# Attention on 128 partitions: 64x32 score products with keys on partitions, and softmax results turned in 32x32 blocks by VectorE

## The chip, the cores and the metric

The kernel runs on one core of one Trainium2 chip. The metric is device time in microseconds from start to end of one execution; the profile shows one execution, and times of several executions stand beside it.

## What is computed

```python
def sm_attn(qq, kk, vv):                  # softmax over the last axis
    s = scale * np.matmul(qq, kk.transpose(0, 1, 3, 2))
    a = np.exp(s - np.max(s, axis=-1, keepdims=True))
    a = a / (np.sum(a, axis=-1, keepdims=True) + 1e-09)
    return np.matmul(a, vv)
# q, k, v: 4 batches, 8 heads, 576 tokens, 64;  p: 4, 8, 32, 64
p_packed = sm_attn(p, k, v)               # 32 packed rows a head
x = sm_attn(q, p_packed, p_packed)        # heads side by side: 2304 x 512
h = x @ w_in                              # 512 x 2048
x = (np.maximum(h, 0) + np.log1p(np.exp(-np.abs(h)))) @ w_out    # 2048 x 512
gate = 1 / (1 + np.exp(-(x @ w_gate)))    # 512 x 1536
out = (gate * (x @ w_val)) @ w_out2       # 1536 x 512
```

All inputs arrive in DRAM: q, k, v, p in float32, the weights in float64.

## The kernel before, in words

The program has three parts that overlap. **Attention** is cut into eight units: unit `u` is batch `u // 2` and half of its heads (four heads). A unit is a Python generator (`attn_unit`) whose `yield`s divide it into 11 stages; `att_tick` moves one unit on by one stage, and up to three units are in flight. **The first expert layer** goes by batch, 256 columns of `w_in` at a time: `emit_h` multiplies, `emit_out1` adds the second product into the tile `xa`, and between its pieces `between` calls `att_tick` and `tick` (one step of weight preparation). The later batches' attention therefore stands between the first batches' products in TensorE's order. **The second expert layer** follows.

Large products split each float32 operand into two float32r parts, so one product is three matmuls (L111 to L113, L641 to L644). Products of the attention, and the transposes, are plain float32; one such matmul is two records in the trace, a transpose one.

A unit before: tokens stand on 96 partitions, six tokens each. GpSimd puts two heads side by side (`by_chunk`, L336), TensorE transposes chunks of 96 tokens (L347), ScalarE copies them out of PSUM (L354). The scores of p (L378) have the 128 rows of four heads' p on partitions and use a left operand with zeros off a head's own block. After the softmax, TensorE turns the result (L412), ScalarE copies it (L413), and 24 products with v (L431) give the packed rows, which ScalarE puts into `bdT`. The scores of q (L455) have tokens on partitions. Their softmax runs in two halves on 96 partitions: VectorE takes the maximum, subtracts, sums and inverts (L465 to L472), ScalarE does the exponential (L469), GpSimd the product (L473). TensorE turns the result (L483), ScalarE and VectorE split it into `A2h` and `A2l`.

The second product of the attention is folded into `w_in`: `Wp` is the packed rows times `w_in` for one batch and 256 columns. `prep_wp_one` (L560) makes it for one batch on 64-column pieces, for columns 0 and 1; `prep_wp_two` (L578) makes it for a pair of batches at once, for columns 2 to 7, and there ScalarE copies to SBUF and GpSimd does both parts of the split (L102, L99).

A weight tile arrives on SyncE's queue (`load_next`) and is converted by three VectorE instructions (L178, L183, L187). Loads of q, k and v (`load_kqv`, L233) take places in `xa` by a table. The order of instructions on each engine is set when the program is built, and each engine runs its own in order; a wait holds up all that stands behind it. The PSUM has four tiles of one bank (`bank1`) and two of two banks (`bank2`).

Of the kernel before, what the change touches and what calls it, by code (L numbers as in the profile page):

```python
# [9 lines left out]
F32 = mybir.dt.float32  # L10
# [10 lines left out]
def attn_moe_moe_kernel(  # L21
# [28 lines left out]
    NC = 6  # L50
    CT = S // NC
# [9 lines left out]
    BAT = (0, 7)  # L61
    ECS = 3
# [5 lines left out]
    VCH = 8  # L68
    VSP = 0
# [13 lines left out]
    # The layers' sums; queries, keys and values before those.  # L83
# [37 lines left out]
    # A weight's float64 words come as pairs of int32, in tiles of 512 columns.  # L121
# [6 lines left out]
    # Some of the second layer's are converted during the first and kept in DRAM.  # L128
# [13 lines left out]
    def load_next():  # L142
# [3 lines left out]
        if XR and key == ("out", 0, 0):  # L146
            # The sums' tile is free until the first of them.
            t = xa[:, : 2 * DM].bitcast(I32).rearrange("p (n t) -> p n t", t=2)
        else:
            t = raw.tile([P, KD * P, 2], I32, tag="raw", name="raw_" + nm)  # L150
        a = c * CF + f * P
        if nm in ("out", "o2"):
            nc.sync.dma_start(t.rearrange("p n t -> p (n t)"), w32[nm][a : a + P, :])
        else:
# [37 lines left out]
    def convert_split(key, pool, shape, tag, bufs):  # L192
# [8 lines left out]
    # Queries, keys and values take the accumulators' slots before those are  # L201
    # needed; a slot's next tile is loaded behind its last use.
    PLACE = {
        0: "345", 1: "621", 2: "345", 3: "634", 4: "563", 5: "456",
        6: "565", 7: "656",
    }
    plan = deque(
        (nm, u, int(s)) for u in range(2 * B) for nm, s in zip("kqv", PLACE[u])
    )
    if PO:  # L210
        first = sorted((plan.popleft() for _ in range(6)), key=lambda x: PO.index(x[0] + str(x[1])))
        plan.extendleft(reversed(first))
    kqv, busy = {}, {}
    KQV = 4 * NC * D

    def load_kqv():
        while plan and plan[0][2] not in busy:
            nm, u, tag = plan.popleft()
            b, g = divmod(u, 2)
            if tag == 6:  # L220
                t = att.tile([CT, KQV], F32, tag="acc6", name=f"{nm}{u}")
            else:
                t = xa[:CT, KQV * tag : KQV * (tag + 1)]
            src = {"k": k, "q": q, "v": v}[nm][b, 4 * g : 4 * g + 4]
            if nm == "v" and u >= VCH:
                t = t.rearrange("p (c h d) -> p c h d", c=NC, h=4)
                for hh in range(4):
                    nc.sync.dma_start(t[:, :, hh], src[hh].rearrange("(r c) d -> r c d", c=NC)) if VSP else None
                if not VSP:
                    nc.sync.dma_start(t, src.rearrange("h (r c) d -> r c h d", c=NC))  # L230
            else:
                t = t.rearrange("p (h c d) -> p h c d", h=4, c=NC)
                nc.sync.dma_start(t, src.rearrange("h (r c) d -> r h c d", c=NC))  # L233
# [35 lines left out]
    for t in pT:  # L269
        nc.gpsimd.memset(t, 0.0)  # L270
# [87 lines left out]
    def attn_unit(u):  # L358
# [119 lines left out]
        for _ in range(BLANK):  # L478
            yield
# [567 lines left out]
```

## Time and profile before

| | |
|---|---|
| time, median of three executions | 874.96 us (873.7 to 875.31) |
| span of the profiled execution | 870.4 us |
| TensorE busy (matmul records) | 841.8 us, 97% |
| VectorE busy | 618.2 us, 71% |
| ScalarE busy | 401.8 us, 46% |
| GpSimd busy | 473.4 us, 54% |

The span runs from the first to the last instruction of the one execution that was profiled; no time of its own is given for that execution. The three timed executions lie 3.3 to 4.9 us above the span. Busy time is the union of an engine's records; a TensorE record is longer than the distance to the next one, since matmuls overlap.

### The profile page before, as it was taken

How to read it: one execution, taken by the hardware profiler on the slowest of the kernel's cores; microseconds unless marked ns; L12 is line 12 of the kernel's file. 1: busy time of each engine (PE TensorE's matmuls, PEld its weight loads, DVE VectorE, ACT ScalarE, POOL GpSimd, SP SyncE). 2: the span in 40 equal slices, each digit the busy share in tenths (PEclk: the TensorE clock that was granted, in tenths of full speed). 3: DMA queues.
4: the chain of work that ended last, by engine and by line, in shares of the span. 5: the costliest groups of instructions: out<-in, count | busy, mean ns of one | idle time of the engine just before them, and what ended most of it. 6: DMA issues, size and time to landing. Idle time of an engine off the chain costs nothing.

```text
span 870.4 us, 15541 instructions
## 1 busy us (share of the span) xinstructions
PE 841.8 (97%) x6064; PEld 790.2 (91%) x6064; DVE 618.2 (71%) x1047; ACT 401.8 (46%) x721; POOL 473.4 (54%) x455
## 2 busy tenths in 40 slices
PE   6889999999999999999999999999989999999997
PEld 5778989989999999999989999999979999999995
DVE  2886556747476857758798688898898746667665
ACT  4557565656666656677633431232342432322210
POOL 4544333254646455476469787886983534436400
PEclk9979999999999999999999999999999999999999
DMA  9774320112032402310056555644424213213004
GB/s 242 197 207 113 83 66 19 49 49 73 25 98 91 134 1 98 110 43 1 2 154 193 162 168 153 188 128 150 153 75 143 82 47 92 67 43 109 14 1 109
DMA packets 58010, 85.55 MB, mean 98 GB/s; under 512 B 6353, under 2 KB 39249, under 8 KB 57937
## 3 DMA queue, kind: packets, MB, share of 16 engines
q1 hardware_dynamic: 57648, 84.49, 33.8%
q8 instruction: 48, 0.79, 0.4%
q14 instruction: 26, 0.20, 0.1%
q10 hardware_dynamic: 288, 0.07, 0.0%
HBM read 65.67 MB, written 18.87 MB: 97 GB/s over the span
## 4 chain that ended last, share of the span: by engine, by line
PE 81%; DVE 9%; DMA 3%; ACT 3%; POOL 2%; issue 1%; SPq 0%; DVEq 0%; ACTq 0%; POOLq 0%
PE bank L113 9%; PE bank L112 9%; PE bank L111 9%; PE ps L641 6%; PE ps L642 6%; PE ps L644 6%; PE ps L967 5%; PE ps L965 5%; PE ps L966 5%; PE ps L113 3%; PE ps L111 3%; PE ps L112 3%; PE ps L578 2%; PE ps L455 2%; DVE aop L99 2%
## 5 line engine op out<-in xcount | busy, mean ns | idle before, releaser
L111 PE MATMUL bank<-aop,BH 128*128 128x288 f32 x672 | 198.7, 296 | 2.8 <-DVE work L918 1.0
L112 PE MATMUL bank<-aop,BH 128*128 128x288 f32 x672 | 197.9, 295 | 1.0 <-DVE aop L99 0.9
L113 PE MATMUL bank<-aop,BL 128*128 128x288 f32 x672 | 198.7, 296 | 0.1
L99 POOL TENSOR_TENSOR ghl<-g,ghl 128x576 fp32r<-128x576 f32 x64 | 93.7, 1465 | 138.8 <-ACT ghl L106 134.4
L649 DVE TENSOR_TENSOR xa<-xa,ps 128x288 f32<-128x288 f32 x224 | 98.1, 449 | 76.9 <-PE ps L644 76.8
L641 PE MATMUL ps<-ghl,woh 128*128 128x288 f32 x512 | 149.2, 306 | 2.5 <-DVE xa L649 2.4
L642 PE MATMUL ps<-ghl,wol 128*128 128x288 f32 x512 | 143.9, 296 | 0.0
L111 PEld LDWEIGHTS bank<-aop,BH 128*128 128x128 f32 x672 | 126.2, 188 | 8.0 <-issue 1.2
L112 PEld LDWEIGHTS bank<-aop,BH 128*128 128x128 f32 x672 | 126.4, 188 | 5.1 <-DVE aop L99 1.6
L113 PEld LDWEIGHTS bank<-aop,BL 128*128 128x128 f32 x672 | 126.5, 188 | 0.4 <-POOL BL L99 0.4
L99 POOL TENSOR_TENSOR BL<-cv,BH 128x512 fp32r<-128x512 f32 (+1 forms) x96 | 117.6, 1241 | 7.2 <-ACT BH L106 6.1
L644 PE MATMUL ps<-ghl,woh 128*128 128x288 f32 x512 | 109.4, 295 | 0.0
L641 PEld LDWEIGHTS ps<-ghl,woh 128*128 128x128 f32 x512 | 96.9, 189 | 6.1 <-DVE xa L649 2.1
L642 PEld LDWEIGHTS ps<-ghl,wol 128*128 128x128 f32 x512 | 97.0, 190 | 0.5
L918 DVE TENSOR_TENSOR work<-work,bank 128x576 f32<-128x576 f32 (+1 forms) x100 | 71.0, 725 | 29.0 <-PE bank L113 28.4
L965 PE MATMUL ps<-oh,gv 128*128 128x512 f32 x216 | 84.6, 392 | 1.3 <-DVE xa L973 0.8
L966 PE MATMUL ps<-ol,gv 128*128 128x512 f32 x216 | 84.8, 393 | 0.0
L967 PE MATMUL ps<-oh,gv 128*128 128x512 f32 x216 | 84.7, 393 | 0.0
L644 PEld LDWEIGHTS ps<-ghl,woh 128*128 128x128 f32 x512 | 82.7, 189 | 0.0
L973 DVE TENSOR_TENSOR xa<-xa,ps 128x512 f32<-128x512 f32 x90 | 61.5, 683 | 27.4 <-PE ps L967 26.9
L947 ACT ACTIVATE work<-bank 128x576 f32<-128x576 f32 (+1 forms) x25 | 15.8, 633 | 137.2 <-DVE bank L918 137.2
L113 PE MATMUL ps<-A2h,wpl 128*128 128x288 f32 x256 | 76.3, 298 | 2.9 <-POOL wpl L99 2.0
(121 smaller groups left out, 1745.8 us busy)
## 6 DMA issues: line engine op xcount, KB each, us to landing
cv<-B SPq DMA_DIRECT2D x52, 256.0 KB, 2.7
B<-cv SPq DMA_DIRECT2D x48, 256.0 KB, 2.9
raw_in<-in_moe_w_in_dram SPq DMA_DIRECT2D x16, 512.0 KB, 4.0
raw_out<-in_moe_w_out_dram SPq DMA_DIRECT2D x16, 512.0 KB, 3.7
raw_g<-in_moe_w_gate_dram SPq DMA_DIRECT2D x12, 512.0 KB, 4.1
raw_v<-in_moe_w_val_dram SPq DMA_DIRECT2D x12, 512.0 KB, 4.4
raw_o<-in_moe_w_out_dram SPq DMA_DIRECT2D x12, 512.0 KB, 4.2
xa<-in_q_dram SPq DMA_DIRECT2D x6, 576.0 KB, 6.6
```

Of the source, the lines that this page charges most:

```text
L99: eng.tensor_tensor(lo, x, hi.bitcast(F32), op=ALU.subtract)
L111: nc.tensor.matmul(ps, wh, xh, start=first, stop=False)
L112: nc.tensor.matmul(ps, wh, xl, start=False, stop=False)
L113: nc.tensor.matmul(ps, wl, xh, start=False, stop=last)
L641: nc.tensor.matmul(out_, wh[:, ms], gh[:, f], start=f == 0, stop=False)
L642: nc.tensor.matmul(out_, wl[:, ms], gh[:, f], start=False, stop=False)
L644: nc.tensor.matmul(out_, wo_hl[c, f][0][:, ms], gl[:, f], start=False, stop=f == 1)
L649: nc.vector.tensor_tensor(dst, dst, out_, op=ALU.add)
L918: nc.vector.tensor_tensor(to, x, y, op=ALU.add)
L965: nc.tensor.matmul(bank, gh[:, ts_], oh, start=f == 0, stop=False)
L966: nc.tensor.matmul(bank, gh[:, ts_], ol, start=False, stop=False)
L967: nc.tensor.matmul(bank, gl[:, ts_], oh, start=False, stop=f == 1)
```

## The change

Tokens now stand on 128 partitions: four heads by 32 groups of 18 tokens. A load of q, k or v is one run of 1152 numbers per partition (18 tokens), and the loads' places are taken from whatever is free, two extra tiles included. TensorE transposes 128x128 chunks (18 a unit for q and k together, where there were 24); two tokens of 64 lie in one chunk, so the halves of the partitions (`e`) hold even and odd tokens. Scores of p and of q are eight products of a 64x32 left operand each (`scores`): the four heads go to four groups of 32 output partitions, and the two halves `e` read different halves of the input partitions and write different banks. Both score tiles have the 32 keys on partitions. VectorE turns 32x32 blocks (`nc.vector.transpose`): once after the first softmax (in place of L412 and L413), once ahead of the second and once behind it (in place of L483). The second softmax runs in one piece of 128x576. The product with v is 72 products of 32 rows each in place of 24 of 96; the packed rows lie in `ppT` without zeros. `Wp` is made of 64x32 pieces too (`prep_wp`), eight for a batch and 256 columns, for a pair of batches at once except at the very first; it takes two banks, and VectorE does the second part of the split in all cases. The split of `A2l` goes from VectorE to GpSimd, `by_chunk` and the zero fills go away. A tile of `w_in` arrives in two DMAs. An output tile of 128 tokens is written by four DMAs of 32 rows each in place of two or three. The stages of a unit stay 11; `BLANK` goes, a second unit now starts at stage 2 of the first (`G0`), and what is needed ahead of a stage (`NEEDS`) is renumbered.

```diff
-    NC = 6
-    CT = S // NC
+    NR = 32
+    NC = S // NR // 2
...
+        elif nm == "in":
+            for g in range(2):
+                nc.sync.dma_start(
+                    t[64 * g : 64 * g + 64].rearrange("p (k n) t -> p k (n t)", k=KD),
...
-                nc.sync.dma_start(t, src.rearrange("h (r c) d -> r h c d", c=NC))
+            nc.sync.dma_start(t, src.rearrange("h (r c) d -> (h r) (c d)", r=NR))
...
+    def turned(src, dst):
+        for i in range(0, NC, 3):
             ps = bank1()
+            for c in range(i, i + 3):
                 nc.tensor.transpose(
+                    ps[:, (c - i) * P : (c - i + 1) * P], src[:, c * P : (c + 1) * P], ident
                 )
+            o = dst[:, i : i + 3].rearrange("p c n -> p (c n)")
+            nc.scalar.activation(o, ps[:, : 3 * P], AF.Copy)
+            yield
...
+    def scores(lhsT, xT, to):
+        for e in range(2):
+            r = slice(64 * e, 64 * e + 64)
+            for h in range(4):
+                n = slice(NK * h, NK * h + NK)
+                nc.tensor.matmul(
+                    to[e][n], lhsT(r, h), xT[r, :, n], start=True, stop=True
+                )
...
+        nc.vector.tensor_scalar(a1, a1, mx[:, 3:4], None, op0=ALU.mult)
+        a1T = att.tile([P, 2 * NC, NK], F32, tag="a1T", bufs=2, name="a1T")
+        nc.vector.transpose(a1T.rearrange("p c n -> p (c n)"), a1)
...
+        pp = [bank1() for _ in range(2)]
+        for e in range(2):
             for c in range(NC):
+                for h in range(4):
+                    r = slice(NR * h, NR * h + NR)
                     nc.tensor.matmul(
+                        pp[h // 2][64 * (h % 2) : 64 * (h % 2) + 64, :NK],
+                        vt[r, c, e, :], a1T[r, e * NC + c, :],
+                        start=e == c == 0, stop=(e, c) == (1, NC - 1),
...
+        for h in range(4):
+            for x in range(2):
+                copy(
+                    PPA[h // 2], ppT[64 * x : 64 * x + 64, b, 4 * g + h, :],
+                    pp[h // 2][64 * (h % 2) : 64 * (h % 2) + 64, :NK],
+                )
+        yield
+        s2 = [bank1() for _ in range(2)]
+        scores(
+            lambda r, h: ppT[r, b, 4 * g + h, :], qT,
+            [x[:, :HS].rearrange("p (c r) -> p c r", r=NR) for x in s2],
+        )
...
+            nc.vector.transpose(
+                a2[:, e * NC : (e + 1) * NC].rearrange("p c n -> p (c n)"), s2[e][:, :HS]
             )
+        nc.vector.tensor_reduce(m2[:, 0], a2, op=ALU.max, axis=AX.X)
...
+        nc.vector.transpose(A2, a2.rearrange("p c n -> p (c n)"))
+        nc.scalar.activation(A2h[b][:, g], A2, AF.Copy)
+        split_lo(nc.gpsimd, A2l[b][:, g], A2, A2h[b][:, g])
...
+    def prep_wp(items):
...
+        for i, (b, c) in enumerate(items):
+            for h in range(4):
+                for t in range(2):
+                    r = slice(64 * t, 64 * t + 64)
+                    nc.tensor.matmul(
+                        ps[t][NK * h : NK * h + NK, i], ppT[r, b, 4 * t + h, :],
+                        w_in_f[c][r, h, :], start=True, stop=True,
+                    )
...
         for t in range(2):
+            nc.scalar.activation(hi[:, :, t], ps[t], AF.Copy)
+            split_lo(nc.vector, lo[:, :, t], ps[t], hi[:, :, t])
...
-                n = min(e - a, CT - r)
-                nc.sync.dma_start(outv[b, cc, r : r + n, :], acc[a - t0 : a - t0 + n])
-                a += n
+                ee, cc = divmod(r // NR, NC)
+                nc.sync.dma_start(outv[b, ee, cc], acc[a - t0 : a - t0 + NR])
+                a += NR
```

In TensorE's order, unit 3 (the second of batch 1) shows what a unit's products become. Before, its product with v, its transposes of q and the next stage (names: out, left and right tile; x is the count of matmuls):

```order
L431 MATMUL ps_639<-a1T,xa 64x32 x24
L347 MATMUL ps_675<-ident,x 128x96 x3
L347 MATMUL ps_680<-ident,x 128x96 x3
L455 MATMUL ps_692<-bdT,qT 96x64 x6
L455 MATMUL ps_708<-bdT,qT 96x64 x6
```

In the changed kernel, at the like place, between two groups of the first layer's products:

```order
L330 MATMUL ps_636<-kT,pT 32x288 x8
L373 MATMUL ps_663<-a1T,own_86 64x32 x2
L373 MATMUL ps_664<-a1T,own_86 64x32 x2
L373 MATMUL ps_663<-a1T,own_86 64x32 x2
...
L317 MATMUL ps_747<-ident,xa 128x128 x3
L330 MATMUL ps_753<-qT,ppT 32x288 x2
L330 MATMUL ps_754<-qT,ppT 32x288
```

One run of 24 matmuls into one tile became 36 rows of two matmuls that alternate between two tiles (the row with "..." stands for 33 of them), and the scores went from 12 matmuls of 64 columns to eight of 288.

On VectorE, at the start, the three instructions that convert the first tile of `w_in` (raw_in is the arrived tile) stood before between the two softmax of the units 0 and 1:

```order
L398 TENSOR_SCALAR a_187<-a_187,mx 128x576
L386 TENSOR_REDUCE mx<-ps_217 128x1
L387 TENSOR_SCALAR mx<-mx 128x1
L178 TENSOR_SCALAR w_in<-raw_in 128x4x128
L393 TENSOR_SCALAR mx<-mx 128x1
L183 SCALAR_TENSOR_TENSOR w_in<-raw_in,w_in 128x4x128
```

In the changed kernel they stand in unit 1's second softmax:

```order
L395 STREAM_TRANSPOSE a_471<-ps_461 128x288
L413 STREAM_TRANSPOSE A_456<-a_336 128x576
L395 STREAM_TRANSPOSE a_471<-ps_462 128x288
L398 TENSOR_REDUCE m_472<-a_471 128x18
L189 TENSOR_SCALAR w_in<-raw_in 128x4x128
L399 TENSOR_TENSOR a_471<-a_471,m_472 128x576
L194 SCALAR_TENSOR_TENSOR w_in<-raw_in,w_in 128x4x128
```

They moved behind nearly all of the first two units' work, and SyncE issues the load of that tile behind ten loads of q, k and v in place of six.

On SyncE, the last rows before:

```order
L982 DMA out_dram<-xa 96x512 x2
L982 DMA out_dram<-xa 32x512
L982 DMA out_dram<-xa 64x512 x2
L982 DMA out_dram<-xa 32x512
L982 DMA out_dram<-xa 96x512
```

and in the changed kernel:

```order
L672 DMA cv<-B_7695 128x512
L672 DMA cv<-B_7695 128x256
L672 DMA cv<-B_7695 128x512 x3
L874 DMA out_dram<-xa 32x512 x36
```

The last nine tiles of 128 tokens are written by 36 DMAs where there were 18.

## Rows read from the trace of the kernel before

**Rows 1.** The page's head and busy times.

```profile
span 870.4 us, 15541 instructions
PE 841.8 (97%) x6064; PEld 790.2 (91%) x6064; DVE 618.2 (71%) x1047; ACT 401.8 (46%) x721; POOL 473.4 (54%) x455
```

**Rows 2.** Windows: stretch, length, each engine's busy time, clock, DMA share, GB/s.

```profile
0.00:37.30 37.30, 27.42 (x270) 22.72 (x270) 17.26 (x46) 18.08 (x51) 16.30 (x25) 1.00 0.99 240
37.30:59.90 22.60, 18.92 (x155) 15.50 (x154) 18.65 (x30) 13.81 (x34) 11.91 (x10) 0.79 0.74 196
59.90:150.10 90.20, 90.01 (x906) 83.71 (x905) 54.70 (x128) 56.37 (x127) 35.26 (x35) 1.00 0.30 75
150.10:405.00 254.90, 251.40 (x1821) 245.95 (x1821) 172.67 (x336) 165.36 (x261) 136.12 (x116) 0.99 0.21 66
```

**Rows 3.** TensorE's timeline, single bursts: start, length, instructions.

```profile
17.69 0.82 PE L412 MATMUL ps<-ident,a 128*96 128x128 f32 x6
...
63.16 0.29 PE L112 MATMUL ps<-A2l,wph 128*128 128x288 f32 x1
63.29 0.29 PE L113 MATMUL ps<-A2h,wpl 128*128 128x288 f32 x1
63.52 1.59 PE L431 MATMUL ps<-a1T,xa 96*64 96x32 f32 x48
65.04 0.40 PE L641 MATMUL ps<-ghl,woh 128*128 128x288 f32 x1
...
66.44 2.18 PE L455 MATMUL ps<-bdT,qT 128*96 128x64 f32 x24
...
73.39 0.66 PE L347 MATMUL ps<-ident,x 96*128 96x96 f32 x6
...
74.71 2.10 PE L378 MATMUL ps<-kT,pT 128*128 128x288 f32 x8
```

**Rows 4.** The same timeline, where `Wp` is made.

```profile
79.67 1.95 PE L560 MATMUL ps<-w_in,bdT 128*64 128x256 f32 x16
81.55 0.40 PE L111 MATMUL ps<-A2h,wph 128*128 128x288 f32 x1
...
170.14 1.03 PE L578 MATMUL ps<-w_in,bdT 128*128 128x256 f32 x4
...
171.14 0.29 PE L642 MATMUL ps<-ghl,wol 128*128 128x288 f32 x1
```

**Rows 5.** Groups by line and form, 59.9 to 150.1 us: count, busy us, mean ns.

```profile
L455 PE MATMUL ps<-bdT,qT 128*96 128x64 f32 x120 | 10.9, 247 | 0.0
L378 PE MATMUL ps<-kT,pT 128*128 128x288 f32 x32 | 8.5, 408 | 0.0
```

**Rows 6.** Groups by line and form, whole span, VectorE, with idle time before.

```profile
L386 DVE TENSOR_REDUCE mx<-ps 128x1 f32<-128x576 f32 x8 | 6.0, 747 | 17.7 <-PE ps L378 17.7
L398 DVE TENSOR_SCALAR a<-a,mx 128x576 f32<-128x576 f32 x8 | 4.3, 539 | 0.2
L465 DVE TENSOR_REDUCE m<-ps 96x12 f32<-96x384 f32 x16 | 8.8, 549 | 5.1 <-PE ps L455 5.1
L99 DVE TENSOR_TENSOR wpl<-ps,wph 128x512 fp32r<-128x512 f32 x8 | 5.5, 684 | 5.6 <-ACT wph L564 5.6
```

**Rows 7.** Timeline at the start, where `w_in` and the first products come.

```profile
19.48 0.43 DVE L178 TENSOR_SCALAR w_in<-raw_in 128x512 int32<-128x512 int32 x1 [1.86 <-DMA raw_in<-in_moe_w_in_dram]
...
35.54 1.08 PE L560 MATMUL ps<-w_in,bdT 128*64 128x256 f32 x8
...
37.32 0.40 PE L111 MATMUL ps<-A2h,wph 128*128 128x288 f32 x1
```

**Rows 8.** Timeline at the end: SyncE's output DMAs and VectorE's last addition.

```profile
855.84 11.44 SPq L982 DMA_DIRECT2D out_dram<-xa  x18
...
865.72 0.69 DVE L973 TENSOR_TENSOR xa<-xa,ps 128x512 f32<-128x512 f32 x1 [0.67 <-PE ps L967]
```

**Rows 9.** TensorE's waits from 150 to 405 us: total, times, longest.

```profile
PE ps L113 <- POOL wpl L99: 2.0, 1, 2.0
```

More of the change, by code (lines that the diff above doesn't have):

```diff
@@ L199, in convert_split, with place @@
         return hi, lo
[L203 to L212, printed above, removed]
-    kqv, busy = {}, {}
-    KQV = 4 * NC * D
+    KQV = 2 * NC * D
+    NEXT = 2
+    own = [att.tile([P, KQV], F32, name=f"own{i}") for i in range(NEXT)]
+    plan = deque((nm, u) for u in range(2 * B) for nm in "kqv")
+    first = sorted((plan.popleft() for _ in range(6)), key=lambda x: PO.index(x[0] + str(x[1])))
+    plan.extendleft(reversed(first))
+    kqv, busy = {}, {}
+    def place(u):
+        for tag in [*range(2 * (u // 2), 2 * B), *range(2 * B, 2 * B + NEXT)]:
+            if tag not in busy:
+                return tag
+        return None
     def load_kqv():
-        while plan and plan[0][2] not in busy:
-            nm, u, tag = plan.popleft()
+        while plan and (tag := place(plan[0][1])) is not None:
+            nm, u = plan.popleft()
             b, g = divmod(u, 2)
[L220 to L223, printed above, removed]
+            t = own[tag - 2 * B] if tag >= 2 * B else xa[:, KQV * tag : KQV * (tag + 1)]
             src = {"k": k, "q": q, "v": v}[nm][b, 4 * g : 4 * g + 4]
[L225 to L232, printed above, removed]
-                nc.sync.dma_start(t, src.rearrange("h (r c) d -> r h c d", c=NC))
+            nc.sync.dma_start(t, src.rearrange("h (r c) d -> (h r) (c d)", r=NR))
             if nm == "k" and u + 1 < 2 * B:
@@ L263, in attn_moe_moe_kernel @@
     make_identity(nc, ident)
[L266 to L271 removed]
+    ppT = ph1.tile([P, B, H, NK], F32, name="ppT")
     A2h = [big.tile([P, 2, S], F32R, tag="big", name=f"A2h{b}") for b in range(B)]
@@ L368, in attn_unit @@
-        kt = kqv.pop(("k", u))
-        kT = att.tile([P, 2, S], F32, tag="kT", bufs=1, name="kT")
-        tr_pair(kt, 0, kT, nc.scalar)
-        yield
-        tr_pair(kt, 1, kT, E1)
+        pT = att.tile([P, P], F32, tag="pT", bufs=2, name="pT")
+        nc.scalar.activation(pT, px[:, :P], AF.Copy)
+        kT = att.tile([P, NC, P], F32, tag="kT", bufs=1, name="kT")
+        yield from turned(kqv.pop(("k", u)), kT)
         done_kqv("k", u)
-        yield
         s1 = bank2()
-        for hf in range(2):
-            for j in range(2):
-                nc.tensor.matmul(
-                    s1[:, hf, :HS],
-                    pT[u % 2][:, P * j : P * j + P],
-                    kT[:, j, hf * HS : (hf + 1) * HS],
-                    start=j == 0,
-                    stop=j == 1,
-                )
+        scores(
+            lambda r, h: pT[r, NK * h : NK * h + NK], kT,
+            [s1[:, e, :HS].rearrange("p (c r) -> p c r", r=NR) for e in range(2)],
+        )
@@ L417, in attn_unit @@
-        yield
-        vt = kqv.pop(("v", u))
-        pp = bank1()
-        for j in range(2):
+        qT = att.tile([P, NC, P], F32, tag="qT", bufs=2, name="qT")
+        yield from turned(kqv.pop(("q", u)), qT)
+        done_kqv("q", u)
+        vt = kqv.pop(("v", u)).rearrange("p (c e d) -> p c e d", c=NC, e=2)
+        pp = [bank1() for _ in range(2)]
+        for e in range(2):
             for c in range(NC):
-                if u >= VCH:
+                for h in range(4):
+                    r = slice(NR * h, NR * h + NR)
@@ L545, in prep_wo @@
             yield
-    def wp_tiles():
-        return [
-            ph1.tile([P, 2, CF], F32R, tag="wp" + y, bufs=4, name="wp" + y) for y in "hl"
-        ]
-    def prep_wp_one(b, c):
-        half, odd = divmod(b, 2)
-        wt = w_in_f[c]
-        hi, lo = wp_tiles()
-        ps = bank1().rearrange("p (t n) -> p t n", t=2)
-        for t in range(2):
-            for par in range(2):
-                r = slice(64 * (odd ^ par), 64 * (odd ^ par) + 64)
-                nc.tensor.matmul(
-                    ps[r, t, :], bdT[:, 4 * half + 2 * t + par, r], wt[:, 2 * t + par, :],
-                    start=True, stop=True,
-                )
-        nc.scalar.activation(hi, ps, AF.Copy)
-        split_lo(nc.vector, lo, ps, hi)
-        Wp[b, c] = (hi, lo)
-        yield
@@ L827, in attn_moe_moe_kernel @@
             if b:
-                for cc in range(2):
-                    jobs.appendleft((f"wp{b}{1 - cc}", prep_wp_one(b, 1 - cc)))
+                jobs.appendleft((f"wp{b}0", prep_wp([(b, 0), (b, 1)])))
         if (b, c) == (3, 0):
```

202 lines of the change are left out of this document (36 added, 166 removed).

## The prediction

> **What bounds the kernel now.** I read the head of the page first: TensorE is busy 97% of 870.4 us, VectorE 71%, the others about half [rows 1]. So a TensorE record that goes is worth its time only where TensorE doesn't wait. The table of windows says where that is [rows 2]. Up to 37.3 us the DMA engines are full (share 0.99, 240 GB/s) and TensorE is mostly between short bursts. From 37.3 to 59.9 us it is busy 18.92 of 22.60 us, at a granted clock of 0.79. From 59.9 to 150.1 us it is busy 90.01 of 90.20 us at full clock: there the attention of later units lies between the first layer's products, and every removed record shortens the run. From 150.1 to 405 us it is busy 251.40 of 254.90.
>
> A record's length isn't its price, since matmuls overlap. The price is the distance between starts, and the timeline of bursts gives it [rows 3]: a burst's length less one record's own, over its count less one. L378 is 2.10 us for eight records of 0.408 us each [rows 5]: 1.69/7 = 0.241 us. L455: (2.18 - 0.25)/23 = 0.084. L347: 0.66 for six, with 0.25 for one as in L455: 0.082; L412 (0.82 for six, 0.29 for one, the length of a 128-row record beside it): 0.106; L431: (1.59 - 0.22)/47 = 0.029, 0.22 being my estimate of one of its records. Full products start 0.13 apart (63.16, 63.29). The burst of L431 begins 0.23 behind the record before it instead of 0.13, and the record behind it starts 1.52 us after it, 0.13 more than 48 times 0.029: leaving and re-entering the full array costs about 0.22 us.
>
> **The change part by part.** *A unit on TensorE.* Before: 24 records of L347 at 0.082 (1.97), eight of L378 at 0.241 (1.93), six of L412 (0.64), 48 of L431 (1.39), 24 of L455 (2.02), six of L483 at 0.082 (0.49), one switch (0.22): 8.6 us. After: 18 transposes of 128x128 at L412's 0.106, 1.91. Each score is eight products of 288 columns, 16 records, on eight pieces of the array: if all eight run at once, two rounds of 0.241, and 0.05 for the spread, 0.53; twice 1.06. The product with v is 144 records of L431's width. One by one, at 0.029, they take 4.18 us; four at once, 1.05.
>
> What the trace says on pieces is one comparison [rows 4]. L578 makes `Wp` with the whole array: four records start within 170.14 to 171.14, less the 0.13 of the product behind, 0.87, 0.217 a record. L560 makes it on 64-column pieces for the same 256 columns: (1.95 - 0.38)/15 = 0.105 a record (0.38 estimated for one). So two pieces that differ in their output partitions run side by side, at no loss. That pieces on different input partitions do so too, and four or eight at once, no row shows. For the product with v I take two at a time, 2.09 us, because that is the number the rows show; for scores and `Wp`, whose pieces stream 256 or 288 columns and so last longer than any spread of the starts, I take all eight, with one record by one record as the other end. With three switches (0.66) the unit costs 5.7: 2.9 us less.
>
> The stretch from 59.9 to 150.1 holds 32 records of L378 (four units' worth) and 120 of L455 (five) [rows 5]; by the costs above about 4.6 units. Saving **-13.3 us**. Units outside it stand where TensorE waits anyway, and are taken at nothing.
>
> The Trainium skill (TensorE: Matmul & The Clock Gate, Part 3: Packing small matmuls) says that pieces in different row groups run concurrently too, 4 of them at 3.07 times and 16 at 10.6 times the rate; no row here tests it. By it the product with v would be near its lower end, and the time some 4.8 us below my sum.
>
> *Wp.* A pair of batches was 16 records of L560, 1.97 us with its switches, for columns 0 and 1 (three pairs after the start), or eight of L578, 1.74 us, for columns 2 to 7 (twelve pairs). Now each pair is 32 records, four rounds of 0.217 in eight pieces, 0.87 + 0.05 + 0.22 (switch): 1.1 us. 3 x 0.87 + 12 x 0.64 = **-10.2 us**, all where TensorE is full. If only four run at once it is 2.0 a pair, and +3.1 in place of it.
>
> *Who does the split of Wp.* Once after 150 us TensorE waits 2.0 us for GpSimd's `wpl` [rows 9]; that goes to VectorE: **-2**. In turn 24 more `wpl` stand in VectorE's row. Eight of that line waited 5.6 us for ScalarE [rows 6], 0.7 each; behind each are the additions to `xa` that free PSUM banks for TensorE. Nothing lost, where TensorE has a bank in hand, to 24 x 0.7 = 17 us: I take **+1.5**, near the lower end, because eight of them waited before and TensorE stayed at 98 to 99% [rows 2].
>
> *VectorE's transposes.* They are in no row. Bounds: the plain pass over 128x576 in L398, 0.54 us, and the reduction out of PSUM in L386, 0.75 [rows 6]; I take 0.75. A unit gets three passes (two of 576, two of 288): 2.25 us, against which it loses the two-half softmax and a split. At the whole 2.25 the stretch has 54.7 + 4.6 x 2.25 = 65 us of VectorE in 90.2 - 13.3 = 77: 85%. Not the bound on the average, but a unit's chain has two more links, and `xa` additions stand behind them: **+3** (0 to 6).
>
> *The start.* The first tile of `w_in` was there at 19.48 us [rows 7]. It now stands behind four more loads of 590 KB, 2.46 us each at 240 GB/s: about 29 us. Its conversion then goes between unit 1's second softmax, some 4 to 5 us more, 34 us; the first `Wp` was at 35.54 and the first product at 37.32, so the tile is just in time, if units 0 and 1 finish as before. They lose `by_chunk` and gain transposes. **+1** (-2 to +4).
>
> *The end.* SyncE issued the last nine tiles' 18 DMAs in 11.44 us from 855.84 [rows 8], paced by the tiles. Now there are 36. If SyncE takes 0.5 us for each (11.44/18 = 0.64 is an upper end; 0.43 is the lower, at which four DMAs would just keep up with somewhat slower tiles) it is done 18 us after the first, 873.8 in place of 867.28: **+6.2** with a little taken back by earlier first issues (+3.6 to +9.8). Nothing else is there to cover it: VectorE's last addition is at 865.72. The other 27 tiles' writes, if they queue, delay only loads that come early.
>
> **Sum.** -13.3 - 10.2 - 2 + 1.5 + 3 + 1 + 6.2 = -13.8: the profiled execution would go from 870.4 to 856.6. The three timed runs lie 3.3 to 4.9 us above that span, the median 4.6, so the median goes to **861**.
>
> **Rivals.** *Short records are limited by their starts.* If records of 32 columns can't start closer than the 0.029 us of L431, the product with v takes 4.18, a unit saves 0.8, the stretch 3.7: 9.6 more, 871. For it: the row on L431 is the only one with records this short. Against: the pieces are separate, as L560's are. The Trainium skill, in the same page's section "Wait — 56ns, not 53.3ns?", puts the least distance at about 25 ns however short a matmul is; by that 3.6 us a unit, and 868. Chance 0.18.
>
> *Only output columns run side by side.* If pieces that differ in their input partitions take turns, the product with v is 4.18 a unit (+9.6), each score two rounds more (+0.96 a unit, +4.4), each pair of `Wp` 0.87 more (15 times, +13): +27, **888, slower than before**. It decides at half of that, since the sum is -13.8. For it: L560's two pieces had the same input partitions, and no row has others. Against: nothing in the rows but that the columns are independent. 0.14.
>
> *VectorE comes too late.* If its `wpl` waits cost 17 instead of 1.5, and the transposes' links 6 instead of 3, it is 18.5 more, 880. For it: 71% busy already and three jobs in one row; against: the stage's average of 85%. 0.12.
>
> *More than the sum.* If four pieces run at once (-4.8) and the idle 3.7 us of 37.3 to 59.9 us goes with shorter units: 853. 0.06.
>
> **How the numbers follow.** The forecast has 0.5, with 853 to 870 as its own range, from the ends of start, end and transposes. With the first rival, the third and the fourth the range is 852 to 882; the 888 lies outside, with a few hundredths of the rest. A measurement of this kernel tells about 0.2% (1.7 us) from no change. Faster: the forecast 0.46 of 0.5, the first rival 0.14 of 0.18, the fourth 0.06, together 0.66; same: 0.08, the upper ends of those two; slower: 0.14 + 0.12 = 0.26.
>
> **What would show it.** A burst of L373 (144 records) of about 2.1 us, not 4.2 or 1.1; of L330 (16) of 0.5 to 0.75, not 1.2; of L484 (32) of about 1.1, not 2. Transposes on VectorE at 0.75 a 576. The first full product within 3 us of 37. The windows: the stretch with all attention in it some 13 us shorter. At the end one run of 36 DMAs of about 18 us. I am wrong if TensorE in the timeline waits on `wpl` or transposed tiles by more than 5 us in all, if the bursts don't overlap, or if the start is late by more than the conversion of one tile.

## The result, and the profile after

The changed kernel takes 882.36 us (median of 7 runs) where the kernel before took 874.05 on the same chip: a ratio of 1.0095 (95% interval 1.0069 to 1.0121). It is 0.95% slower; 861 and faster was forecast. The profiled execution has a span of 881.4 us, 11.0 more than before. The medians differ by 8.3 us only: executions for which both were noted took 1.7 to 2.2 us longer than their span, so the profiled execution of the kernel before took about 872.4 us (an estimate), less than each of the seven timed here. The 11.0 us that are divided up below are the difference of the two profiled executions.

Line numbers of the changed kernel, as the rows use them: L317 and L337 transpose on TensorE, L330 makes scores, L373 the product with v, L484 `Wp`, L113 to L115 the first product, L535 to L538 the second product of the first layer, L858 to L860 the last product of the second. In some runs they are shifted by a few lines.

The head of its page and its windows (stretch, length, busy time of TensorE, its weight loads, VectorE, ScalarE, GpSimd, then granted clock, DMA share, GB/s) answer to [rows 1] and [rows 2]:

```profile
PE 822.9 (93%) x7040; PEld 753.9 (86%) x7040; DVE 639.6 (73%) x1081; ACT 376.5 (43%) x659; POOL 404.9 (46%) x372
```

```profile
0.00:37.30 37.30, 22.76 (x400) 16.35 (x400) 14.72 (x34) 13.34 (x34) 3.54 (x8) 0.77 0.68 212
37.30:59.90 22.60, 13.83 (x235) 10.38 (x235) 18.68 (x33) 11.82 (x25) 8.60 (x6) 0.65 0.74 202
59.90:150.10 90.20, 82.40 (x1263) 69.55 (x1259) 63.38 (x145) 51.98 (x112) 25.36 (x20) 0.92 0.28 86
150.10:405.00 254.90, 244.64 (x2211) 230.35 (x2204) 184.71 (x358) 148.49 (x236) 98.41 (x74) 1.00 0.23 66
```

TensorE is busy 18.9 us less and the run is longer: TensorE waits more, and runs at half its clock (1.2 in place of 2.4 GHz, granted clock 0.50) more. Up to 37.3 us its granted clock was 1.00 before and is 0.77; from 59.9 to 150.1 us it was 1.00 and is 0.92, with 7.8 us not busy where there were 0.2.

Like records of the two traces tell where the 11 us arise. They are the first record of the first product, its 279th of 768, the last records of the first layer's second product, and the first of the second layer's last product. In the changed kernel:

```profile
44.49 0.61 PE L113 MATMUL ps<-A2h,wph 128*128 128x288 f32 x1
...
221.38 0.29 PE L115 MATMUL ps<-A2h,wpl 128*128 128x288 f32 x1
...
445.44 0.43 PE L538 MATMUL ps<-ghl,woh 128*128 128x288 f32 x2
...
480.98 0.39 PE L858 MATMUL ps<-oh,gv 128*128 128x512 f32 x1
```

and before, behind the 37.32 of [rows 7]:

```profile
221.17 0.29 PE L113 MATMUL ps<-A2h,wpl 128*128 128x288 f32 x1
...
440.49 0.43 PE L644 MATMUL ps<-ghl,woh 128*128 128x288 f32 x2
...
474.71 0.39 PE L965 MATMUL ps<-oh,gv 128*128 128x512 f32 x1
```

The first full product starts at 44.5 us in place of 37.3 (+7.2). The 279th record starts at 221.4 in place of 221.2, so those 177 us take 7.0 us less than the like stretch before. The second product's last record starts at 445.6 in place of 440.6, the second layer's last product at 481.0 in place of 474.7: 6.1 us lost since 221. Nothing more is lost until VectorE's last addition; the last 4.7 us come behind it. 7.2 - 7.0 + 6.1 + 4.7 = 11.0. Single executions vary: e1 and e4 below run the same program up to 640 us and have these two first records at 45.1 and 222.9, and at 43.1 and 220.9.

The 7.0 us are less than TensorE's work fell. Between the first and the 279th record its busy time is 15.4 us less, and 8.4 of them came back as idle time (15.4 us in place of 7.0; the changed kernel first, then before):

```profile
44.50:221.40 176.90, 161.46 (x2150) 141.18 (x2150) 129.95 (x272) 102.44 (x201) 57.73 (x42) 0.93 0.31 87
```

```profile
37.30:221.20 183.90, 176.88 (x1538) 164.28 (x1538) 121.45 (x254) 112.87 (x230) 78.80 (x71) 0.96 0.31 84
```

The longest of the new waits there are these (total us, times, longest):

```profile
PE ps L484 <- DVE w_in L198: 2.8, 1, 2.8
PE ps L373 <- issue: 2.6, 2, 2.3
PE ps L113 <- ACT wph L490: 2.3, 2, 1.4
```

The bursts that the forecast priced are these (TensorE's timeline; start, length, count of records at the end):

```profile
73.53 2.30 PE L373 MATMUL ps<-a1T,xa 32*64 32x32 f32 x144
75.76 0.40 PE L535 MATMUL ps<-ghl,woh 128*128 128x288 f32 x1
...
88.21 0.72 PE L330 MATMUL ps<-kT,pT 64*32 64x288 f32 x16
88.86 0.33 PE L337 MATMUL ps<-ident,p 128*128 128x128 f32 x1
...
89.44 1.09 PE L484 MATMUL ps<-w_in,ppT 64*32 64x256 f32 x32
90.47 0.40 PE L535 MATMUL ps<-ghl,woh 128*128 128x288 f32 x1
```

From start to the next start: 2.23 us for the product with v, 0.65 for a score, 1.03 for a pair's `Wp`. With 18 transposes at 0.106 a unit is 5.4 us, without switches. A switch is about 0.2 us a burst: the starts just ahead of a pair's `Wp` and those of the two records behind it are 0.22 and 0.24 apart in place of 0.13 (228.13 and 228.35, 229.38 and 229.61). With it a pair costs 1.2 us and a unit with three switches 6.0. VectorE's transposes (count, busy us, mean ns, idle time before):

```profile
L395 DVE STREAM_TRANSPOSE a<-ps 128x288 f32<-128x288 f32 x16 | 7.0, 463 | 11.2 <-PE ps L330 11.2
L361 DVE STREAM_TRANSPOSE a1T<-a 128x576 f32<-128x576 f32 x8 | 6.2, 776 | 0.2
```

TensorE's longest waits over the whole span (total us, times, longest) show what took the place of the saved work:

```profile
PE ps L484 <- DVE w_in L198: 11.7, 2, 8.9
...
PE ps L535 <- DVE wpl L101: 5.8, 6, 2.0
PE ps L373 <- issue: 4.0, 3, 2.3
```

The first waits are for the conversion of `w_in`. Before, TensorE had no wait for it among those the view lists. It had none for "issue" either, which is time in which nothing that the profile shows was waited for.

The first two units, on TensorE (start, length, in brackets the idle time before):

```profile
15.66 3.40 PE L373 MATMUL ps<-a1T,xa 32*64 32x32 f32 x144
...
24.52 3.42 PE L373 MATMUL ps<-a1T,xa 32*64 32x32 f32 x118
29.32 0.95 PE L373 MATMUL ps<-a1T,xa 32*64 32x32 f32 x26 [1.39 <-issue]
...
42.87 1.11 PE L484 MATMUL ps<-w_in,ppT 64*32 64x256 f32 x16 [8.90 <-DVE w_in L198]
```

The burst that takes 2.23 us later takes 3.3 and 5.7 here, at half clock from 16.5 us on and in the second with a pause inside. On VectorE, the conversion of the first two tiles, which the first `Wp` needs (L189, L194, L198 for each), stands behind unit 1's transposes of the scores and between the steps of its second softmax:

```profile
32.57 0.48 DVE L395 STREAM_TRANSPOSE a<-ps 128x288 f32<-128x288 f32 x1 [1.03 <-PE ps L330]
...
34.78 0.42 DVE L189 TENSOR_SCALAR w_in<-raw_in 128x512 int32<-128x512 int32 x1
...
37.70 0.69 DVE L198 SCALAR_TENSOR_TENSOR w_in<-raw_in,w_in 128x512 int32<-128x512 int32 x1
...
41.37 0.78 DVE L413 STREAM_TRANSPOSE A<-a 128x576 f32<-128x576 f32 x1 [1.05 <-POOL a L407]
42.07 0.65 DVE L198 SCALAR_TENSOR_TENSOR w_in<-raw_in,w_in 128x512 int32<-128x512 int32 x1
```

No idle time for the DMA stands before L189: the tiles had come, and waited in VectorE's row. The second tile's last step stands behind unit 1's last transpose (L413), for which VectorE waited 1.05 us for GpSimd.

At the end one group of DMAs, 17 us for 36, beside VectorE's last addition, as in [rows 8]:

```profile
862.13 17.00 SPq L874 DMA_DIRECT2D out_dram<-xa  x36
```

```profile
872.01 0.69 DVE L866 TENSOR_TENSOR xa<-xa,ps 128x512 f32<-128x512 f32 x1 [0.67 <-PE ps L860]
```

### The profile page after: what moved, and what is told of

The parts are those of the page before. It is cut to its first block, busy times and chain, and to the rows that moved or that the text cites. A ratio compares the mean times of both kernels' runs of the same rounds, so it can differ in the third digit from the quotient of the medians.

```text
span 881.4 us, 17355 instructions
## 1 busy us (share of the span) xinstructions
PE 822.9 (93%) x7040; PEld 753.9 (86%) x7040; DVE 639.6 (73%) x1081; ACT 376.5 (43%) x659; POOL 404.9 (46%) x372
## 4 chain that ended last, share of the span: by engine, by line
PE 76%; DVE 14%; ACT 4%; issue 3%; DMA 2%; POOL 1%; SPq 0%; DVEq 0%; POOLq 0%; ACTq 0%
PE bank L115 9%; PE bank L113 9%; PE bank L114 9%; PE ps L535 6%; PE ps L536 6%; PE ps L538 5%; PE ps L860 5%; PE ps L859 5%; PE ps L858 5%; PE ps L115 3%; PE ps L113 3%; PE ps L114 3%; PE ps L373 2%; DVE xa L543 2%; DVE aop L101 1%
## 5 line engine op out<-in xcount | busy, mean ns | idle before, releaser
L113 PE MATMUL bank<-aop,BH 128*128 128x288 f32 x672 | 199.0, 296 | 4.0 <-DVE work L823 1.7
L115 PE MATMUL bank<-aop,BL 128*128 128x288 f32 x672 | 198.7, 296 | 0.0
L535 PE MATMUL ps<-ghl,woh 128*128 128x288 f32 x512 | 149.4, 306 | 8.7 <-DVE wpl L101 5.8
L543 DVE TENSOR_TENSOR xa<-xa,ps 128x288 f32<-128x288 f32 x224 | 96.1, 448 | 60.1 <-PE ps L538 59.4
L113 PEld LDWEIGHTS bank<-aop,BH 128*128 128x128 f32 x672 | 126.3, 188 | 9.6 <-issue 1.4
L115 PEld LDWEIGHTS bank<-aop,BL 128*128 128x128 f32 x672 | 126.6, 188 | 0.0
L535 PEld LDWEIGHTS ps<-ghl,woh 128*128 128x128 f32 x512 | 96.9, 189 | 21.1 <-DVE wpl L101 8.0
L538 PE MATMUL ps<-ghl,woh 128*128 128x288 f32 x512 | 110.4, 296 | 0.0
L858 PE MATMUL ps<-oh,gv 128*128 128x512 f32 x216 | 84.6, 392 | 1.3 <-DVE xa L866 0.8
L860 PE MATMUL ps<-oh,gv 128*128 128x512 f32 x216 | 84.8, 393 | 0.0
L538 PEld LDWEIGHTS ps<-ghl,woh 128*128 128x128 f32 x512 | 83.2, 189 | 0.1
L113 PE MATMUL ps<-A2h,wph 128*128 128x288 f32 x256 | 78.0, 305 | 3.7 <-ACT wph L490 2.3
L866 DVE TENSOR_TENSOR xa<-xa,ps 128x512 f32<-128x512 f32 x90 | 61.6, 684 | 26.7 <-PE ps L860 26.1
L811 DVE TENSOR_TENSOR bank<-work,bank 128x576 f32<-128x576 f32 (+1 forms) x75 | 54.8, 736 | 32.7 <-PE bank L115 32.4
```

Source lines behind the costliest of these rows:

```text
L113: nc.tensor.matmul(ps, wh, xh, start=first, stop=False)
L115: nc.tensor.matmul(ps, wl, xh, start=False, stop=last)
L535: nc.tensor.matmul(out_, wh[:, ms], gh[:, f], start=f == 0, stop=False)
L538: nc.tensor.matmul(out_, wo_hl[c, f][0][:, ms], gl[:, f], start=False, stop=f == 1)
L543: nc.vector.tensor_tensor(dst, dst, out_, op=ALU.add)
L811: nc.vector.tensor_tensor(to, x, y, op=ALU.add)
```

## The experiments

All start from the changed kernel (1.0095 of the kernel before); ratios are to the kernel before, on the same chip.

**e1_out: fewer output DMAs.**

```diff
-                nc.sync.dma_start(outv[b, ee, cc], acc[a - t0 : a - t0 + NR])
-                a += NR
+                m = min((e - a) // NR, NC - cc)
+                nc.sync.dma_start(outv[b, ee, cc : cc + m], acc[a - t0 : a - t0 + m * NR])
+                a += m * NR
```

> The changed kernel, with the 32-row pieces of an output tile that lie at one stride in DRAM written by one DMA (one or two for a tile in place of four; the bytes are the same). Theory (the end is set by SyncE's issues, 36 in 17 us, 0.47 us each): the last DMA is issued within about 1 us of VectorE's last addition and the run is 4 to 5 us shorter, ratio about 0.995 to the changed kernel. Rival (the writes themselves, in 32-row pieces, take the time): the last write lands when it did, less than 1 us shorter.

Ratio 1.025 (1.0187 to 1.0313): 1.5% slower than the changed kernel, which neither expected. Of the 16.5 us by which its span is longer, 4.5 arise ahead of VectorE's last addition (876.5 in place of 872.0) and 12.0 behind it. The twelve DMAs at the end take longer than the 36 (SyncE's timeline), and the share of the DMA engines from 866 us to the end is 0.25 in the windows, where the changed kernel's is 0.48 from 862 us on:

```profile
866.59 19.40 SPq L875 DMA_DIRECT2D out_dram<-xa  x12
```

The edit changed the form of the DMA as well as the count, so it decides nothing on SyncE's issues. From 872 to 880 us the share stands at 0.26, about what four busy engines of 16 make, and the outermost dimension of the merged DMA is one to four pieces where it was 32 rows. That this dimension decides on how many engines a DMA is spread would fit; it was not tested by itself.

**e4_two_queues: the same DMAs, half of those for the second half of the tokens issued by ScalarE's queue.**

```diff
-                nc.sync.dma_start(outv[b, ee, cc], acc[a - t0 : a - t0 + NR])
+                eng = nc.scalar if ps and a // NR % 2 else nc.sync
+                eng.dma_start(outv[b, ee, cc], acc[a - t0 : a - t0 + NR])
```

> The changed kernel, with every second output DMA of the second half of the tokens issued by ScalarE's queue in place of SyncE's; the DMAs themselves are the same 32-row pieces. Theory (the end is paced by one engine's issues, 0.47 us each): 18 issues on each queue keep up with the tiles (1.36 us each, two issues a queue), the last write is issued within 1.5 us of VectorE's last addition, 4 to 5 us shorter. Rival (the DMA engines take 0.47 us for 64 KB in this form, whoever issues): the writes end as late as before, less than 1 us shorter.

Ratio 1.0019 (0.9993 to 1.0045), span 875.5. Both queues end at 873.1, 0.9 us behind VectorE's last addition (871.57 + 0.69), and the span ends 3.3 us behind it in place of 8.7 in the changed kernel. The DMAs are the same ones, so the end was paced by one queue's issues:

```profile
861.70 11.39 SPq L875 DMA_DIRECT2D out_dram<-xa  x18
```

```profile
861.70 11.44 ACTq L875 DMA_DIRECT2D out_dram<-xa  x18
```

**e3_loads: `w_in` ahead of the last four loads.**

```diff
-    def load_kqv():
-        while plan and (tag := place(plan[0][1])) is not None:
+    def load_kqv(most=99):
+        while most and plan and (tag := place(plan[0][1])) is not None:
+            most -= 1
...
+    load_kqv(6)
+    for _ in range(2):
+        load_next()
     load_kqv()
-    for _ in range(4):
+    for _ in range(2):
         load_next()
```

> The changed kernel, with the first two tiles of w_in loaded behind six loads of q, k and v in place of ten; VectorE's conversions move ahead of the units' second softmax with that. Theory (the late w_in conversion, 8.9 us of wait at the first Wp, delays the first product by 7 us): first full product at 38 to 41 us in place of 44.5, the run 4 to 6 us shorter. Rival (unit 1's own chain is as late, because TensorE's half clock and its pauses in the first two units hold it up): the wait moves from w_in to the softmax result, the first product comes at 43 to 45 us, the run shorter by less than 1.5 us.

Ratio 1.0046 (1.0017 to 1.0075), span 877.3. The first product starts at 36.5 us, even ahead of before, and the conversion begins at 18.99. Unit 1 is as late as in the changed kernel: its product with v still takes 4.93 us, and the next record starts at 30.4 where it started at 30.2. So its lateness reaches the first product only through the conversion that stands behind it. But half of the 8.0 us is given back (4.2 are left at 441 us): the second `Wp` now waits 7.0 us for the second tile pair of `w_in`, where it waited 2.8.

```profile
25.54 4.93 PE L374 MATMUL ps<-a1T,xa 32*64 32x32 f32 x144
...
36.45 0.40 PE L113 MATMUL ps<-A2h,wph 128*128 128x288 f32 x1 [0.29 <-ACT wph L491]
...
63.42 1.11 PE L485 MATMUL ps<-w_in,ppT 64*32 64x256 f32 x16 [6.98 <-DVE w_in L198]
```

**e6_short: the product with v cut to 16 records.**

```diff
-            for c in range(NC):
+            for c in range(1):
                 for h in range(4):
...
-                        start=e == c == 0, stop=(e, c) == (1, NC - 1),
+                        start=e == c == 0, stop=(e, c) == (1, 0),
```

> The changed kernel, with eight of nine token pairs left out of the product with v (16 records a unit in place of 144; the output is not the reference's). If the pauses of TensorE that wait for nothing in the profile (4.0 us in L373 and 1.4 in L330, all next to a packet of the instruction queue) come from the long bursts of short records, they go. By prices alone a unit saves 128 x 0.0155 = 2 us where TensorE is full, about 8 us between 67 and 150 us; by the theory that units at the start also wait on these bursts at half clock and in those pauses (3.4 and 5.7 us for two bursts of 2.2), the first product comes no earlier than its w_in tile allows, 41 to 43 us. In all 6 to 12 us shorter. Rival (the bursts are hidden, the units' chains wait on VectorE): under 4 us shorter.

The run leaves out eight ninths of that product. Ratio 0.9898 (0.9846 to 0.9951), span 865.4: 16 us shorter, above what was expected. The first product comes at 37.2 us, 7.3 earlier, though the loads stand where they stood; the pauses on "issue" are gone; up to the 279th product another 10.7 us are saved (203.4 in place of 221.4). Six units' bursts lie in that stretch, 12 us at 2.0 each, so most of their price is paid there. Later nothing more is gained.

```profile
35.62 1.11 PE L484 MATMUL ps<-w_in,ppT 64*32 64x256 f32 x16 [10.65 <-DVE w_in L198]
...
37.23 0.61 PE L113 MATMUL ps<-A2h,wph 128*128 128x288 f32 x1
```

So these bursts, at the start, were not work that TensorE did while it waited anyway: unit 1's second softmax stood behind them, and the conversion stood behind that.

**e10_fill: TensorE kept busy in its two waits for `w_in`.**

```diff
+        for _ in range({(0, 0): 40, (0, 1): 20}.get(items[0], 0)):
+            nc.tensor.transpose(ps[0][:, 0, :P], ident, ident)
```

> The changed kernel, with 40 and 20 transposes of the identity into the waiting bank ahead of the first and the second Wp, where TensorE waits 8.9 and 2.8 us for w_in; their results are overwritten. Theory (half clock behind those waits costs time: the first 24 products start 0.24 apart in place of 0.133, and so do those from 67.7 to 71.1 us): the clock is at its full level when the products begin, and the run is 2 to 5 us shorter. Rival (what follows waits for VectorE and ScalarE anyway): the clock is higher and the run within 1 us of the changed kernel.

Ratio 1.0056 (1.0025 to 1.0088). The windows show the clock, first three stretches of the changed kernel, then two of them in this one:

```profile
16.51:33.57 17.06, 14.29 (x290) 10.17 (x283) 7.83 (x23) 4.79 (x15) 1.16 (x1) 0.50 0.64 169
44.50:50.64 6.14, 5.47 (x33) 3.93 (x33) 5.15 (x8) 2.78 (x6) 1.28 (x1) 0.50 1.03 310
67.71:71.12 3.41, 3.41 (x16) 3.40 (x16) 2.52 (x7) 1.05 (x3) 0.00 (x0) 0.50 0.92 342
```

```profile
44.50:50.64 6.14, 5.99 (x44) 3.70 (x42) 4.12 (x9) 3.33 (x7) 1.30 (x1) 0.83 0.98 295
67.71:71.12 3.41, 3.36 (x27) 3.13 (x25) 2.37 (x7) 1.33 (x3) 1.50 (x2) 1.00 0.80 287
```

The first product starts 0.3 us earlier, the 279th 3.8 us (217.6). From the one to the other it is 173.4 us, where the changed kernel takes 176.9 and e1 and e4, the same program up to there, 177.8 and 177.7: the half clock and the waits that the filling changed cost 3.5 us or somewhat more there, as the theory had it. In the time of the whole run that isn't shown: by the end of the profiled run 1.2 us are left (one more spell at half clock came at 401 us), and the ratios differ by 0.4%, with intervals that overlap. That is close to what the rival expected.

**e2_pool and e2_later: who computes `wpl`, and when.** The first puts it on GpSimd, the second one step later on VectorE, for columns 2 to 7.

```diff
+                x = new_cv().rearrange("p (i n) -> p i n", i=2)
+                nc.scalar.activation(x, ps[t], AF.Copy)
+                split_lo(nc.gpsimd, lo[:, :, t], x, hi[:, :, t])
```

```diff
         for t in range(2):
             nc.scalar.activation(hi[:, :, t], ps[t], AF.Copy)
+        if items[0][1] >= 2:
+            yield
+        for t in range(2):
             split_lo(nc.vector, lo[:, :, t], ps[t], hi[:, :, t])
```

> The changed kernel, with the second part of the split of Wp for columns 2 to 7 on GpSimd again (ScalarE copies PSUM to SBUF for it once more). Theory (wpl on VectorE waits for ScalarE, and the additions to xa that free PSUM banks stand behind it: 12 starts of the second product 6.3 us late between 221 and 446 us): those waits go, 5 to 7 us shorter. Rival (VectorE's row is not what holds the banks, TensorE only waits elsewhere): within 1.5 us of the changed kernel. Second rival: GpSimd comes later than VectorE did, some us longer.

> The changed kernel, with wpl still on VectorE but one step later in its row for columns 2 to 7, so that ScalarE has had time for the first part. Theory (the cost is VectorE standing idle for ScalarE, 0.7 us at a time): most of the 6.3 us goes, 3 to 6 us shorter. Rival (the cost is wpl's own time on VectorE, 0.75 us each, ahead of the additions to xa): 0 to 2 us shorter; then the run with wpl on GpSimd gains and this one doesn't.

Ratios 1.0055 (1.0027 to 1.0083) and 1.0093 (1.0061 to 1.0126): the second changes nothing, the first at most a little (its interval overlaps the changed kernel's). From the 279th product to the first layer's last record it is 222.4 us with GpSimd, 223.0 one step later, 224.2 in the changed kernel (226.0 and 224.3 in e1 and e4, the same program up to there), 219.4 before. With GpSimd the wait only has another name (waits of TensorE from 223 to 446 us; for the changed kernel, from 221 to 446 us, they were 5.0 for `wpl` and 1.8 for `xa`):

```profile
PE ps L542 <- DVE xa L550: 4.0, 8, 1.2
PE ps L542 <- ACT cv L497: 2.2, 1, 2.2
```

**e5_scratch: conversions without a PSUM bank in the first layer.**

```diff
-        if (b, c) == CPC:
-            cps[0] = CPS > 0
...
+    cps[0] = CPS > 0
     while pend:
```

> The changed kernel, with the conversions of weights writing straight to SBUF in all of the first layer, where from batch 1's column group 2 on they take one of the four single PSUM banks for their intermediate. Theory (the new Wp takes two of the four banks at once and holds them until VectorE's wpl, so that together with the conversion's bank the second product has one left; who computes wpl matters little, as the two runs before showed): the 12 late starts of the second product between 221 and 446 us (6.3 us) shrink to under 2, 3 to 6 us shorter. Rival (VectorE itself is late with its additions): within 1.5 us.

Ratio 1.0216 (1.0159 to 1.0274): 1.2% slower. By 229.3 us it has lost 7.9 us already, and it waits for VectorE's `xa` more (4.4 us in the second product, 3.4 in `Wp`). The edit moved VectorE's conversions too, so it could not tell the theories apart.

**e9_halves: `Wp` in two steps of four pieces, one bank at a time.**

```diff
+        for t in range(2):
+            ps = bank1().rearrange("p (i n) -> p i n", i=2)[:, :n]
+            r = slice(64 * t, 64 * t + 64)
+            for i, (b, c) in enumerate(items):
+                for h in range(4):
...
+            split_lo(nc.vector, lo[:, :, t], ps, hi[:, :, t])
+            yield
```

> The changed kernel, with Wp made in two steps of four pieces (one half of the input partitions each, one PSUM bank at a time) in place of one step of eight pieces in two banks. Theory (the second product starts late between 221 and 446 us because Wp takes two of the four single banks at once until VectorE has read both): its late starts behind the first product's records, 6.3 us there, fall under 2 us; the records of Wp cost about 1.1 us more a pair (four pieces at a time, two switches), so 9 to 10 us more work in that stretch, and the run is between 1 us shorter and 4 us longer. Rival (the banks don't matter): the waits stay, and the run is 8 us or more longer.

Ratio 1.0156 (1.0103 to 1.021): about 5 us longer, between what the theory (at most 4) and the rival (8 or more) expected. Its timeline shows a pair's `Wp` in two bursts, 0.067 us a record where eight pieces took 0.034 (1.09/32):

```profile
230.71 1.07 PE L486 MATMUL ps<-w_in,ppT 64*32 64x256 f32 x16
232.70 1.07 PE L486 MATMUL ps<-w_in,ppT 64*32 64x256 f32 x16
```

And the wait for `wpl` from 223 to 452 us is all but gone, while `xa` waits grew from 1.8 to 3.4:

```profile
PE ps L535 <- DVE xa L543: 3.4, 4, 1.3
PE ps L535 <- DVE wpl L101: 0.3, 1, 0.3
```

The late starts fell, from 6.8 to 3.7 us, and the wait that went is the one for `wpl`, which fits the two banks held at once. Under 2 us in all, as the theory had it, was too much. The edit also makes the step longer on TensorE, which gives VectorE more time; the two aren't told apart.

**e8_three and e11_three: edits together.** e8 has e3, e4 and e5; e11 has e3, e4 and e2_pool.

> The changed kernel with three edits: w_in's first two tiles loaded behind six loads, conversions without a PSUM bank in the first layer, and the last output DMAs on two queues. If the three losses are separate, they add up: 4 + 4 + 4.5, that is 12 to 13 us shorter than the changed kernel, at 0.993 to 0.997 of the time of the kernel before. If the middle waits only move to other places or the two queues share a limit: 4 to 8 us shorter, still at or above the kernel before.

> The changed kernel with the three edits that shortened it: the first two tiles of w_in loaded behind six loads, the last output DMAs on two queues, wpl of columns 2 to 7 on GpSimd. If they are separate they add up, 4.1 + 5.6 + 1.5 = 11 us shorter than the changed kernel, 0.997 to 1.001 of the kernel before. If the earlier start only lengthens the waits in the middle, 7 us shorter and 1.002 to 1.006 of it.

e8: 1.0102 (1.0057 to 1.0147), with e5 in it, which alone lost 1.2%. e11: 871.3 us, **0.9945** (0.9914 to 0.9976), 0.55% shorter than the kernel before. Against the changed kernel it is 11 us shorter by the medians and 13 by the ratios: the three gains add up. Its first product is at 36.1 us and the run ends 4.5 us behind the last product's last record (before 5.1, changed kernel 9.8).

## Why the prediction was wrong

**Where the forecast and the trace part.** Against the forecast's terms, in the two profiled executions: the start +7.2 where +1 was set; from there to the 279th record -7.0 where units, six pairs of `Wp` and the wait for `wpl` were to give -13.3 - 4.5 - 2 = -19.8; from there to 481 us +6.1 where nine pairs were to give -5.8; the end +4.7 where +6.2 was set. For VectorE 4.5 were allowed in all. So the two stretches in which records were to be removed miss by some 20 us together, the start by 6.

**The cheaper records were there.** A unit costs 6.0 us on TensorE with its switches (5.7 forecast), a pair's `Wp` 1.2 (1.1 forecast). Eight pieces do run side by side, on different input partitions too: e9, with half of them at a time, takes twice as long a record. The product with v came at 2.23 (2.09 taken, ends 1.05 and 4.18), so neither of the two rivals on TensorE held. Its 144 records are 0.0155 us a record. By the floor of about 25 ns that the Trainium skill states (TensorE: Matmul & The Clock Gate, "Wait — 56ns, not 53.3ns?") it would have been 3.6 us; the measurement decides against it for separate pieces. VectorE's transposes took 0.78 and 0.46 us (0.75 a 576, and 0.38 for 288, taken).

**The start failed first.** The step "Units outside it stand where TensorE waits anyway, and are taken at nothing", with the start at +1 (-2 to +4), measured +7.2. It was on condition that units 0 and 1 finish as before, and they didn't: the new bursts are not beside the chain there but in it. Packed rows, scores and second softmax of unit 1 wait for them, at half clock and with pauses. The tiles of `w_in` were there in time, but their conversion, which the forecast saw go between the steps of that softmax, turned unit 1's delay into a delay of the first product. The first `Wp` needs two tiles, and their conversion took 7.9 us there (34.78 to 42.72), where 4 to 5 were counted for the first. The loss takes both: with the bursts cut (e6), or with the tiles ahead (e3), the first product starts at 37.2 or 36.5 us.

**The full stretch did not stay full.** From "busy 90.01 of 90.20 us" the forecast took that "every removed record shortens the run". In the changed kernel TensorE is busy 82.40 of those 90.20 us. With its own work shorter, other waits came to the front: up to 221 us, of 15.4 us less work 8.4 came back as idle time, for `w_in`, for ScalarE's `wph`, on "issue" and in shorter waits. That is the same step once more: a term for what TensorE would then wait for was missing.

**The clock had no term.** Before, TensorE's clock fell once in the first 150 us (0.79 in the second window of [rows 2]). The changed kernel is at half clock from 16.5 to 33.6 us, and in several spells more up to 84.8 us, two of which the windows above show; TensorE waited or had pauses ahead of them. The long bursts are not the only cause: e6, without them, still had 0.80 and 0.73 in the first two windows. e10 showed about 3.5 us of the cost up to 221 us.

**The middle term was taken in a wrong form.** For `wpl` on VectorE +1.5 was set, up to 17 for VectorE standing still. Moving it (e2_later) or taking it off VectorE (e2_pool) gave 0 to 2 us in that stretch; making `Wp` with one bank at a time (e9) took the wait for it away. The second product (L535) doesn't read `wpl`; what it waits for there is the PSUM bank that `wpl` reads. Two of four are held until then. The forecast spoke of a bank in hand, but not of the two that `Wp` itself takes. Between 221 and 481 us 6.1 us were lost where nine pairs of `Wp` were to save 0.64 each.

**The end was right in kind.** +6.2 forecast, 4.7 measured: 0.47 us an issue, not 0.5, and the run ended 2.2 us behind the last issue in place of 3.1 before. e4 shows the cause. The writes of the first half of the tokens are those of nine tiles, not of "27". The step from the span to the median was off too: +4.6 taken, +1.0 measured (882.36 over 881.4).

Of the rivals the third, VectorE too late at 880, came nearest in time, but not by its price: it set 17 us for `wpl`, and TensorE waited 5.8 for it, while VectorE's conversion of `w_in` held it up 11.7. Two of the forecast's own signs of being wrong came: more than 5 us of waits on `wpl`, and a start late by more than the conversion of one tile. What stays open: why TensorE pauses on "issue" inside the bursts (below), how the 8.4 us up to 221 divide between pauses, late copies and late weights, and how the 6.1 us divide between banks and late `xa` additions.

## What to carry to other kernels

Price a cheaper product at the start-up chain and at the full stretch apart: where an engine waits, a longer or slower burst on the chain is paid in full, even if the same edit saves time elsewhere. In a full stretch, ask what the engine will wait for once its work is shorter; here more than half of the saved busy time came back as idle time. When an edit makes one step of several, count the PSUM banks it holds at once and for how long, and write the order of the loads and conversions anew. Look at what is left idle after the last computation: here 36 small DMAs on one queue took back 4.7 of the 7.0 us that the cheaper products had gained.

## What the runs showed of the hardware

Three things were not expected. Pieces of 32 input rows start 0.0155 us apart on the average, half the distance of L431 in [rows 3]. Output DMAs of one stride more, with up to 128 rows in place of 32, were slower for the same bytes: twelve took 19.40 us to issue where 36 took 17.00, at half the share of the DMA engines. And TensorE's pauses on "issue" in the changed kernel (4.0 us in L373, 1.4 in L330, gone in e6) end 1.2 to 1.6 us after a 16 KB packet of the instruction queue has come (for one, 26.7 to 27.8, with the start at 29.32); most fall in or right behind stretches in which the DMA engines are fully used by loads. That the code arrives late for a long run of short records fits that, but it was not tested by itself.
